# Storing a result tile that lies in two batches: one transfer over both, or two transfers of 64 rows

## The chip, the cores and the metric

The kernel runs on one core of one Trainium2 chip. The metric is the device time of one execution in microseconds (us). The core has TensorE (PE, with its weight loads as PEld), VectorE (DVE), ScalarE (ACT), GpSimd (POOL) and SyncE (SP). SP computes nothing: here it issues transfers, in program order, to 16 DMA engines.

## The reference

Block-sparse attention over 4 batches, 8 heads, 768 positions of 64 values, in blocks of 32 positions, and then a feed-forward network on the 3072 x 512 result.

```python
scores = scale * np.matmul(q, k.transpose(0, 1, 3, 2))
mask = np.abs(blk_i - blk_j) <= window              # window = 1
mask = mask | (blk_i == 0) | (blk_j == 0) | (blk_i == n_blocks - 1) | (blk_j == n_blocks - 1)
for qb in range(n_blocks):
    for kb in sampled_blocks[qb]:                   # 3 sampled blocks for each block of queries
        mask[qb * block:(qb + 1) * block, kb * block:(kb + 1) * block] = True
scores = np.where(mask, scores, -1000000000.0)
attn = softmax(scores)                              # over the last axis
x = (attn @ v).transpose(0, 2, 1, 3).reshape(B * S, H * D)
h = x @ w_in                                        # 512 x 2048
g = np.where(h > 0.0, h, alpha * (np.exp(np.minimum(h, 0.0)) - 1.0))
return (g @ w_out).astype(np.float32)               # 2048 x 512
```

## The kernel before

The work is cut into 24 units of 128 rows, four blocks of 32 query rows each. There are three kinds. In 20 units two neighbouring blocks of one batch stand beside the same two blocks of the next batch ("two batches"): partitions 0 to 63 of a tile belong to one batch, 64 to 127 to the other. In 2 units all four blocks are of one batch. 2 special units hold the first and the last block of both batches, whose rows see all keys. `attention` makes the scores (`s`, line 788), the exponentials (`e`), their 16-bit high and low parts (`p`, lines 820 to 824), turns `p` round (`pT`, line 825) and multiplies by the values (`w` or `av`, line 837). The result, normalised, is turned round too (`xT`). `ffn` takes two units at a time: the first layer `h` (line 885), the ELU on ACT and DVE (`fe`, lines 893 to 897), `g`, the second layer `o` (line 908).

From unit 4 on the turning is done by DMA transposes (line 377), issued by SP like every load and store. Loads of queries (line 642), keys (578), values (590), staged values (730 and others) and the stores of results all stand in SP's one order.

The result of a unit leaves PSUM as `ro` (line 918, on ACT or DVE, whichever the planner takes) and is stored by `move` (lines 624 to 642). There is a single `ro` buffer, so the next `ro` waits until the store before has landed. The last unit's result uses a `fe` buffer instead. `far` is the output seen as batch, position, column; `tile_` is the 128 x 512 tile in fp32, 256 KB, with rows of 2 KB.

The first store is issued 202.5 us into the span of the profiled execution.

The order on all engines comes from a planner, `Plan.order`, before the program is built. It plays the program forward with a cost for each operation on each engine that may do it, and hands out operations by priority; what it takes for an operation's cost changes which one it hands out next. For a store it takes a cost on SP and 0.9 of DMA time (lines 920 and 921). The costs are the planner's own; they decide the order and nothing else.

Of the kernel before, what the change touches and what calls it, by code (L numbers as in the profile page):

```python
# [225 lines left out]
def kernel(  # L226
# [15 lines left out]
    BLK = 32  # L242
# [21 lines left out]
    plan = Plan(rooms)  # L264
# [6 lines left out]
    def buf(tag, shape, dtype, pool=None):  # L271
        def make():
            made[0] += 1
            return (pool or sb).tile(
                shape, dtype, tag=tag, bufs=rooms[tag], name=f"{tag}{made[0]}")
        return Buf(tag, make)
# [18 lines left out]
    def scaled(eng, dst, src, scale=1.0):  # L295
        if eng == "ACT":
            nc.scalar.activation(dst, src, AF.Copy, scale=scale)
        elif scale == 1.0:
            ENG[eng].tensor_copy(dst, src)  # L299
        else:  # L300
            ENG[eng].tensor_scalar(dst, src, scale, None, op0=ALU.mult)
# [319 lines left out]
    def unit(u):  # L621
        return units[u]

    def move(u, dram, tile_, store=False):

        g, i, blocks = unit(u)
        if store:
            far = dram.rearrange("(b t) e -> b t e", b=B)
        else:
            far = dram.rearrange("b h t d -> b t h d")  # L630
        b, two = 2 * g + blocks[0][0], blocks[0][0] != blocks[3][0]
        if i and not two:
            parts = [(far[b, i * BLK : (i + 4) * BLK], tile_)]
        elif i and store:
            parts = [(far[b : b + 2, i * BLK : (i + 2) * BLK], tile_)]
        elif i:
            parts = [(far[b + x, i * BLK : (i + 2) * BLK], tile_[64 * x : 64 * x + 64]) for x in range(2)]
        else:
            parts = [(far[2 * g + x, n * BLK : (n + 1) * BLK], tile_[BLK * j : BLK * (j + 1)])
                     for j, (x, n) in enumerate(blocks)]  # L640
        for a, b in parts:
            nc.sync.dma_start(a, b) if store else nc.sync.dma_start(b, a)
# [15 lines left out]
    def attention(u, t, via):  # L658
# [6 lines left out]
        s, n = buf("st2", [P, H, D], F32), buf("n2", [P, H, 2, D], F16)  # L665
        qT, qS = buf("qT", [P, H, P], F16), buf("qS", [P, H, P], F16)
        plan.add({"SP": 0.9 if i0 else 1.8}, tq - 3, lambda e: move(u, q, s.ap), new=[s], dma=1.45, name=f"q{u}")
        split(tq - 1, s, n, lambda: n.ap[:, :, 0, :], lambda: n.ap[:, :, 1, :], QS, True, f"q{u}")
        turn16(tq if u != 1 else t - 0.5, n, lambda: qT.ap, via[0], new=[qT], name=f"qt{u}", bank="s" if u else "o")
# [202 lines left out]
    def ffn(U, t):  # L872
        x = xT[U]
        os = [buf("o", [P, DM], F32, ps) for _ in range(2)]
        for f2 in range(NFC // 2):
            h, e32, g = buf("h", [P, 2, 2 * P], F32, ps), buf("fe", [P, 2, 2 * P], F32), buf("g", [P, 2, 2, 2 * P], F16)
            p0 = t + F2 * f2
            for a in range(2):
                def layer1(e, f2=f2, a=a, h=h):
                    w = wi[2 * f2 + a]  # L880
                    n = 0
                    for cc in range(NCC):
                        cs = slice(cc * P, (cc + 1) * P)
                        for wl, xl in ((0, 0), (0, 1), (1, 0)):
                            nc.tensor.matmul(  # L885
                                h.ap[:, a, :], lhsT=w[:, wl, cs], rhs=x.ap[:, xl, cc, :],
                                start=(n == 0), stop=(n == 3 * NCC - 1))
                            n += 1
                plan.add({"PE": 1.31}, p0 + 1.3 * a, layer1, r=[x, w_ready[2 * f2 + a]],
                         new=[h] if a == 0 else [], w=[h] if a else [], code=24, name=f"h{U}.{f2}")  # L890

            def act3(e, h=h, e32=e32):
                nc.vector.scalar_tensor_tensor(  # L893
                    e32.ap, h.ap, -IH * GS, e32.ap, op0=ALU.mult, op1=ALU.min)
            plan.add({"ACT": 0.57}, p0 + 2.6, lambda e, h=h, e32=e32: nc.scalar.activation(  # L895
                e32.ap, h.ap, AF.Exp, scale=IH), r=[h], new=[e32], name=f"a1{U}.{f2}")
            plan.add({"ACT": 0.68}, p0 + 2.6, lambda e, e32=e32: nc.scalar.activation(  # L897
                e32.ap, e32.ap, AF.Relu, bias=gs_col, scale=-GS), r=[e32], w=[e32], name=f"a2{U}.{f2}")
            plan.add({"DVE": 0.66}, p0 + 2.6, act3, r=[h, e32], w=[e32], port=False, name=f"a3{U}.{f2}")
            plan.add(CAST, p0 + 2.6, margin=MC, fn=lambda e, e32=e32, g=g: scaled(e, g.ap[:, 0], e32.ap), r=[e32], new=[g],  # L900
                     name=f"a4{U}.{f2}")
            plan.add(LO, p0 + 2.6, margin=MO, fn=lambda e, e32=e32, g=g: ENG[e].tensor_tensor(  # L902
                g.ap[:, 1], e32.ap, g.ap[:, 0], op=ALU.subtract), r=[e32, g], w=[g], name=f"a5{U}.{f2}")
            for m in range(2):
                def layer2(e, f2=f2, m=m, g=g, o=os[m]):
                    for f in (2 * f2, 2 * f2 + 1):
                        for n, (gl, wl) in enumerate(((0, 0), (0, 1), (1, 0))):
                            nc.tensor.matmul(  # L908
                                o.ap, lhsT=g.ap[:, gl, f % 2, m * P : (m + 1) * P], rhs=wo[f][:, wl, :],
                                start=(f == 0 and n == 0), stop=(f == NFC - 1 and n == 2))  # L910
                plan.add({"PE": 1.31}, p0 + LAG + 1.3 * m, layer2,
                         r=[g, w_ready[NFC + 2 * f2], w_ready[NFC + 2 * f2 + 1]] + [os[m]] * (f2 > 0),
                         new=[os[m]] if f2 == 0 else [], w=[os[m]] if f2 else [], code=12, name=f"o{U}.{m}.{f2}")
        for m, o in enumerate(os):
            p0 = t + F2 * (NFC // 2 - 1) + LAG + 1.3 * m + 0.5
            tag = "fe" if m and U == NU // 2 - 1 else "ro"
            ro = buf(tag, [P, DM], F32)
            plan.add({"ACT": 0.6, "DVE": 0.65}, p0, lambda e, o=o, ro=ro: scaled(e, ro.ap, o.ap, IO),
                     r=[o], new=[ro], port=False, name=f"ro{2 * U + m}")
            plan.add({"SP": 0.6}, p0, lambda e, u=2 * U + m, ro=ro: move(u, out, ro.ap, True),  # L920
                     r=[ro], dma=0.9, name=f"st{2 * U + m}")

    SHIFT = {"ACT": 0.6, "DVE": 0.7}
# [18 lines left out]
    for U in range(NU // 2):  # L942
        t = F0 + T * U
        for u in (2 * U, 2 * U + 1):
            at = t - LEAD + (T / 2 if U else NEXT) * (u % 2)
            if u == NUP:
                for c in range(NKC):
                    for x in range(2):
                        keys(1, x, c, at - K1 + c, "PE")
                for c in range(NKC):  # L950
                    values(1, c, at - V1 + 5 * c)
            attention(u, at, ("PE", 4, "PE") if u < NPE else (("DMA", "PE")[QP], PP if u < TURNED else 0, ("DMA", "PE")[XP]))
        ffn(U, t)
# [32 lines left out]
```

## Time and profile before

| | us |
|---|---|
| runs: median, lowest, highest of 3 | 816.0, 815.18, 816.61 |
| the profiled execution: its time, its span | 816.94, 814.7 |
| PE busy | 710.6 (87%) |
| DVE busy | 509.7 (63%) |
| ACT busy | 407.6 (50%) |
| POOL busy | 393.9 (48%) |

The span runs from the first to the last instruction of the profiled execution. The execution's own time is 2.2 us longer, and 0.9 us above the median of the runs.

### The profile page before, as it was taken

Reading aid. Unit: us, or ns where it says so; the run is one execution under the profiler, and the core shown is the slowest. Engines: PE = TensorE matmul, PEld = TensorE weight load, DVE = VectorE, ACT = ScalarE, POOL = GpSimd, SP = SyncE. Lnnn points to the kernel's source line nnn. Section 1 sums busy time; section 2 is a strip of 40 time slices with the busy share of each in tenths; the row PEclk is TensorE's granted clock in tenths of the full one; section 3 lists DMA queues with packets and bytes.
Section 4 is the critical chain, followed back from the end, with each engine's and each line's share of the span. In section 5 each row is a group of like instructions: output and inputs, shape, how many; then the busy total and the mean of one; then the engine's idle time right before and its main releaser. Section 6 shows DMA issues by size and latency. Waiting matters only on the chain.

```text
span 814.7 us, 26279 instructions
## 1 busy us (share of the span) xinstructions
PE 710.6 (87%) x11064; PEld 478.8 (59%) x11064; DVE 509.7 (63%) x851; ACT 407.6 (50%) x725; POOL 393.9 (48%) x601
## 2 busy tenths in 40 slices
PE   6445576999999998999899899998999979989993
PEld 3333454667667656567567557666666556656761
DVE  7688787888776855675377567567565456463210
ACT  4588767887546635454465335324434343332220
POOL 2587657686634345743455455535633344322220
PEclk7555577999999999999999999999999999999998
DMA  9898998887958798989748999889587499861000
GB/s 240 262 270 275 275 245 185 216 180 143 183 137 247 150 176 181 146 175 186 153 80 159 116 199 120 158 127 151 93 189 127 67 111 191 133 86 20 27 1 26
DMA packets 216405, 126.33 MB, mean 155 GB/s; under 512 B 173344, under 2 KB 193952, under 8 KB 216288
## 3 DMA queue, kind: packets, MB, share of 16 engines
q1 hardware_dynamic: 211008, 107.09, 68.5%
q0 software_dynamic: 5280, 17.58, 8.4%
q8 instruction: 86, 1.41, 0.8%
q14 instruction: 31, 0.25, 0.1%
HBM read 82.05 MB, written 13.21 MB: 117 GB/s over the span
## 4 chain that ended last, share of the span: by engine, by line
PE 58%; DMA 19%; DVE 7%; issue 6%; SPq 3%; ACT 3%; POOL 2%; POOLq 1%; another core or an unknown queue 1%; DVEq 0%; ACTq 0%
PE h L885 23%; PE o L908 23%; DMA pT<-p 10%; PE s L788 5%; PE w L837 3%; PE av L837 2%; DMA wo<-in_moe_w_out_dram 2%; DMA st<-in_k_dram 2%; PE av L385 1%; DMA out_dram<-ro 1%; DMA vd<-VT 1%; DMA st<-in_v_dram 1%; PE s L385 1%; SPq L377 1%; DMA VT<-vd 1%
## 5 line engine op out<-in xcount | busy, mean ns | idle before, releaser
L885 PE MATMUL h<-xT,wi 128*128 128x256 f16 x2304 | 285.0, 276 | 10.9 <-DVE fe L893 8.0
L908 PE MATMUL o<-wo,g 128*128 128x512 f16 x1152 | 276.5, 383 | 0.5 <-issue 0.5
L885 PEld LDWEIGHTS <-wi 128*128 128x128 f16 x2304 | 220.7, 99 | 61.3 <-issue 10.3
L908 PEld LDWEIGHTS <-g 128*128 128x128 f16 x1152 | 108.1, 98 | 111.3 <-issue 4.8
L822 POOL TENSOR_TENSOR p<-e,p 128x512 f16<-128x512 f32 x94 | 112.1, 1195 | 115.3 <-DVE p L299 61.3
L902 POOL TENSOR_TENSOR g<-fe,g 128x512 f16<-128x512 f32 x69 | 83.2, 1206 | 140.2 <-DVE g L299 121.5
L895 ACT ACTIVATE fe<-h 128x512 f32<-128x512 f32 x96 | 57.2, 596 | 165.8 <-PE h L885 163.1
L817 ACT ACTIVATE e<-s,m 128x256 f32<-128x256 f32 x208 | 86.2, 469 | 82.1 <-POOL p L822 42.6
L893 DVE SCALAR_TENSOR_TENSOR fe<-h,fe 128x512 f32<-128x512 f32 x96 | 65.9, 687 | 73.0 <-ACT fe L897 68.4
L757 POOL COPY kG<-kT 128x128 int32 x264 | 78.2, 339 | 52.1 <-PE s L788 29.8
L799 DVE TENSOR_REDUCE m<-s 128x2 f32<-128x512 f32 x104 | 70.1, 686 | 44.1 <-PE s L788 40.8
L735 POOL DMA_INDIRECT VT<-vd,idx x66 | 65.9, 999 | 27.9 <-issue 10.0
L837 PEld LDWEIGHTS <-pT 128*32 128x32 f16 x3456 | 42.9, 97 | 47.9 <-issue 32.1
L897 ACT ACTIVATE fe<-fe,gs 128x512 f32<-128x512 f32 x96 | 69.3, 722 | 2.4
L846 DVE TENSOR_REDUCE x<-w 128x130 f32<-128x260 f32 x64 | 27.3, 426 | 56.3 <-PE w L837 50.8
L788 PE MATMUL s<-kG,qT 128*32 128x160 f16 x704 | 45.5, 250 | 9.8 <-ACT e L817 6.0
L788 PEld LDWEIGHTS <-qT 128*32 128x32 f16 x1664 | 33.6, 101 | 31.1 <-issue 26.8
L788 PE MATMUL s<-kT,qS 128*32 128x96 f16 (+1 forms) x832 | 49.1, 227 | 0.9 <-issue 0.9
L788 PE MATMUL s<-kT,qT 128*32 128x96 f16 (+1 forms) x832 | 49.0, 228 | 1.0 <-issue 1.0
L299 DVE CAST p<-e 128x512 f16<-128x512 f32 x58 | 33.7, 584 | 24.2 <-DMA pT<-p 11.8
L788 PE MATMUL s<-kG,qS 128*32 128x160 f16 x704 | 44.6, 249 | 4.2 <-DVE qS L299 2.7
L837 PE MATMUL w<-VT,pT 128*32 128x65 f16 (+1 forms) x2048 | 34.4, 208 | 7.4 <-DMA pT<-p 7.1
(134 smaller groups left out, 818.9 us busy)
## 6 DMA issues: line engine op xcount, KB each, us to landing
VT<-vd SPq DMA_DIRECT2D x44, 195.0 KB
VT<-vd SPq DMA_DIRECT2D x22, 390.0 KB
wo<-in_moe_w_out_dram SPq DMA_DIRECT2D x12, 512.0 KB
out_dram<-ro SPq DMA_DIRECT2D x21, 256.0 KB
st<-in_q_dram SPq DMA_DIRECT2D x40, 128.0 KB
wo<-in_moe_w_in_dram SPq DMA_DIRECT2D x9, 512.0 KB
st<-in_moe_w_in_dram SPq DMA_DIRECT2D x7, 512.0 KB
VT<-vd SPq DMA_DIRECT2D x12, 260.0 KB
```

The source lines that it names most:

```text
L735: nc.gpsimd.indirect_dma_start(VT[0:96, 2 * vt.slot, xs[0] : xs[-1] + 1].rearrange("p b x -> p (b x)"), None, d.ap, bass.IndirectOffsetOnA ...
L757: nc.gpsimd.tensor_copy(dst[:, :, r * 16 : (r + 1) * 16], src[:, :, bass.ds(at[r], 16)])
L788: nc.tensor.matmul(dst, lhsT=qq.ap[:, h, j * BLK : (j + 1) * BLK], rhs=mv, start=first, stop=(y == 1 and qq is qS and o0 + w == 256))
L799: nc.vector.tensor_reduce(m.ap[:, 2 * c : 2 * c + 2] if sp else m.ap[:, 6:8], ss[c].ap, axis=AX.X, op=ALU.max, negate=True)
L817: nc.scalar.activation(e32.ap[:, y, :], ss[c].ap[:, y, :], AF.Exp, bias=m.ap[:, 6 + y : 7 + y])
L822: plan.add(LO, t + PITCH * hp + 1, margin=MO, fn=lambda e, e32=e32, p=p: ENG[e].tensor_tensor(p.ap[:, 1, :], flat(e32.ap), p.ap[:, 0, :], ...
L837: nc.tensor.matmul(av.ap[j * BLK : (j + 1) * BLK, y, v0:], lhsT=pts[c].ap[:, pl * 4 + y * 2 + z, j * BLK : (j + 1) * BLK], rhs=VT[:, room, ...
L885: nc.tensor.matmul(h.ap[:, a, :], lhsT=w[:, wl, cs], rhs=x.ap[:, xl, cc, :], start=(n == 0), stop=(n == 3 * NCC - 1))
L893: nc.vector.scalar_tensor_tensor(e32.ap, h.ap, -IH * GS, e32.ap, op0=ALU.mult, op1=ALU.min)
L897: plan.add({"ACT": 0.68}, p0 + 2.6, lambda e, e32=e32: nc.scalar.activation(e32.ap, e32.ap, AF.Relu, bias=gs_col, scale=-GS), r=[e32], w=[ ...
L902: plan.add(LO, p0 + 2.6, margin=MO, fn=lambda e, e32=e32, g=g: ENG[e].tensor_tensor(g.ap[:, 1], e32.ap, g.ap[:, 0], op=ALU.subtract), r=[e ...
L908: nc.tensor.matmul(o.ap, lhsT=g.ap[:, gl, f % 2, m * P : (m + 1) * P], rhs=wo[f][:, wl, :], start=(f == 0 and n == 0), stop=(f == NFC - 1 ...
```

## The change

`move` loses its case for a store of a unit in two batches. Such a store then goes the way that the loads of such a unit always went: two transfers of 64 rows, one for each batch, issued one behind the other. The planner's cost of a store on SP goes from 0.6 to 1.1, for all kinds of units.

```diff
         if i and not two:
             parts = [(far[b, i * BLK : (i + 4) * BLK], tile_)]
-        elif i and store:
-            parts = [(far[b : b + 2, i * BLK : (i + 2) * BLK], tile_)]
         elif i:
             parts = [(far[b + x, i * BLK : (i + 2) * BLK], tile_[64 * x : 64 * x + 64]) for x in range(2)]
         else:
...
-            plan.add({"SP": 0.6}, p0, lambda e, u=2 * U + m, ro=ro: move(u, out, ro.ap, True),
+            plan.add({"SP": 1.1}, p0, lambda e, u=2 * U + m, ro=ro: move(u, out, ro.ap, True),
                      r=[ro], dma=0.9, name=f"st{2 * U + m}")
```

The lines after the first edit stand two lines higher in the changed file, so that line 642 becomes 640 and line 730 becomes 728.

What stands in SP's order, at three places. First, SP at the first store of a unit in two batches (`vd` holds the staged values in DRAM, `VT` those in SBUF, `ro` the result). Before:

```order
L706 DMA VT<-vd_183 64x1040
L642 DMA out_dram<-ro_5378 2x64x512
L730 DMA VT<-vd_175 96x1040
L730 DMA VT<-vd_183 96x1040
L599 DMA vd_191<-st_4360 128x2080
```

And after:

```order
L704 DMA VT<-vd_183 64x1040
L640 DMA out_dram<-ro_5378 64x512 x2
L728 DMA VT<-vd_175 96x1040
L728 DMA VT<-vd_183 96x1040
L599 DMA vd_191<-st_4360 128x2080
```

One issue has become two, and nothing else has moved here. Up to the tenth store of such a unit (at 501.87 us in the trace) the order on every engine is as it was.

Second, SP at and behind that tenth store, before:

```order
L377 DMA_TRANSPOSE pT_11036<-p_10981 128x8x128
L642 DMA out_dram<-ro_11056 2x64x512
L730 DMA VT<-vd_191 96x2080
L377 DMA_TRANSPOSE pT_11148<-p_11054 128x8x128
L377 DMA_TRANSPOSE xT_10598<-xn_11132 128x8x128
L377 DMA_TRANSPOSE pT_11293<-p_11195 128x8x128
```

And after:

```order
L377 DMA_TRANSPOSE pT_11044<-p_10989 128x8x128
L640 DMA out_dram<-ro_11064 64x512 x2
L377 DMA_TRANSPOSE pT_11121<-p_11062 128x8x128
L728 DMA VT<-vd_191 96x2080
L377 DMA_TRANSPOSE xT_10605<-xn_11157 128x8x128
L377 DMA_TRANSPOSE pT_11299<-p_11204 128x8x128
```

The transpose that stood behind the value load now stands ahead of it. From here on the planner's order differs in places on all five engines.

Third, SP at the loads of the second special unit, before:

```order
L377 DMA_TRANSPOSE pT_12980<-p_12923 128x8x128
L703 DMA VT<-vd_191 128x2080 x4
L377 DMA_TRANSPOSE xT_12960<-xn_13159 128x8x128
L703 DMA VT<-vd_191 128x2080
L705 DMA VT<-vd_191 64x2080
L706 DMA VT<-vd_191 64x2080
L642 DMA out_dram<-ro_13111 2x64x512
```

And after:

```order
L377 DMA_TRANSPOSE pT_12981<-p_12932 128x8x128
L640 DMA out_dram<-ro_13095 64x512 x2
L701 DMA VT<-vd_191 128x2080 x4
L377 DMA_TRANSPOSE xT_12978<-xn_13185 128x8x128
L701 DMA VT<-vd_191 128x2080
L703 DMA VT<-vd_191 64x2080
L704 DMA VT<-vd_191 64x2080
```

The store that stood behind seven value loads and a transpose now stands ahead of them.

## Rows read from the trace of the kernel before

**Rows 1.** The page: the busy time of each engine (with its share of the span and its instructions), and the shares of the chain that ended last, by engine.

```profile
PE 710.6 (87%) x11064; PEld 478.8 (59%) x11064; DVE 509.7 (63%) x851; ACT 407.6 (50%) x725; POOL 393.9 (48%) x601
PE 58%; DMA 19%; DVE 7%; issue 6%; SPq 3%; ACT 3%; POOL 2%; POOLq 1%; another core or an unknown queue 1%; DVEq 0%; ACTq 0%
```

**Rows 2.** Busy time by stretch: the stretch, its length, then busy us and instructions of PE, PEld, DVE, ACT and POOL, the granted clock of PE, the share of the 16 DMA engines that was busy, and GB/s.

```profile
200.00:500.00 300.00, 283.65 (x4635) 190.93 (x4633) 192.95 (x336) 148.00 (x265) 145.28 (x224) 0.99 0.86 160
500.00:803.00 303.00, 289.39 (x3999) 189.04 (x3997) 155.72 (x256) 111.01 (x206) 118.37 (x145) 0.99 0.65 104
803.00:813.50 10.50, 0.00 (x0) 0.00 (x0) 0.00 (x0) 0.00 (x0) 0.00 (x0) 0.67 0.13 47
```

**Rows 3.** SP's last two issues (start, length of the issue), both stores of units in two batches, and SP's last wait at the program's end (us in total, times, longest).

```profile
800.68 0.52 SPq L642 DMA_DIRECT2D out_dram<-ro  x1
802.04 0.52 SPq L642 DMA_DIRECT2D out_dram<-fe  x1
...
SPq L981 <- DMA out_dram<-fe: 5.1, 1, 5.1
```

**Rows 4.** Two stores of 256 KB side by side. The first is the special unit's, in four transfers of 32 rows: SP's issue of the four, the stretch 759.5 to 762 (columns as in rows 2), and in it the DMA share in 40 slices and the queue's packets, MB and share.

```profile
759.00 1.74 SPq L642 DMA_DIRECT2D out_dram<-ro  x4
759.50:762.00 2.50, 2.50 (x25) 2.24 (x24) 0.00 (x0) 0.00 (x0) 0.00 (x0) 1.00 0.40 105
DMA  0000095893205559621057973305389521000000
q1 hardware_dynamic: 192, 0.26, 40.1%
```

**Rows 5.** The second is the next one, of a unit in two batches in one transfer, issued at 762.87: the stretch 763.9 to 770.4 and its queue. The last line is the DMA share in 40 slices from 813.0 to 814.7, behind the last store of the program.

```profile
763.90:770.40 6.50, 6.50 (x56) 5.24 (x55) 3.25 (x6) 2.64 (x4) 2.36 (x3) 1.00 0.14 43
q1 hardware_dynamic: 130, 0.26, 12.5%
DMA  0202020200000000000000000000000000000000
```

**Rows 6.** SP's issues behind two such stores, in order of time (start, length of the issue), and the issue of all transposes of `p` (least, median, most ns; first and last start).

```profile
448.76 0.60 SPq L642 DMA_DIRECT2D out_dram<-ro  x1
449.46 5.17 SPq L377 DMA_TRANSPOSE pT<-p  x1
...
501.87 0.59 SPq L642 DMA_DIRECT2D out_dram<-ro  x1
...
503.06 5.80 SPq L377 DMA_TRANSPOSE pT<-p  x1
...
L377 SPq DMA_TRANSPOSE pT<-p x72: 1231/1408/6158, 160.9 to 731.2; - x72
```

**Rows 7.** Transfers in the chain that ended last (start of the issue, us until it had landed): a transpose with no store just ahead, two with one, a store for which the next `ro` waited, and two loads behind a store.

```profile
644.94 3.65 DMA pT<-p
650.57 10.23 DMA pT<-p
503.06 11.74 DMA pT<-p
373.62 9.46 DMA out_dram<-ro
388.22 9.39 DMA st<-in_k_dram
261.69 9.19 DMA st<-in_v_dram
```

**Rows 8.** PE's idle times that end with something late behind a store, in order of time (idle time and what ended it in brackets).

```profile
272.56 0.53 PE L837 MATMUL av<-VT,pT 128*32 128x130 f16 x32 [0.59 <-ACT pT L297]
389.74 0.62 PE L385 MATMUL s<-ident,n 128*128 128x128 f16 x8 [0.64 <-DVE n L497]
399.11 0.62 PE L385 MATMUL s<-ident,n 128*128 128x128 f16 x8 [3.09 <-DVE n L497]
463.22 0.53 PE L837 MATMUL w<-VT,pT 128*32 128x130 f16 x32 [3.38 <-DMA pT<-p]
514.84 0.53 PE L837 MATMUL w<-VT,pT 128*32 128x130 f16 x32 [0.74 <-DMA pT<-p]
568.48 0.54 PE L837 MATMUL w<-VT,pT 128*32 128x130 f16 x32 [1.38 <-DMA pT<-p]
660.85 0.71 PE L837 MATMUL av<-VT,pT 128*32 128x130 f16 x32 [2.79 <-DMA pT<-p]
718.15 1.25 PE L885 MATMUL h<-xT,wi 128*128 128x256 f16 x5 [3.17 <-DVE fe L893]
726.07 0.53 PE L837 MATMUL w<-VT,pT 128*32 128x130 f16 x32 [0.47 <-DMA pT<-p]
```

**Rows 9.** Waits for the `ro` buffer, from 200 us on, in total, times, longest; then DVE around one of them.

```profile
DVE ro L301 <- DMA out_dram<-ro: 22.6, 5, 8.9
ACT ro L297 <- DMA out_dram<-ro: 4.7, 2, 2.8
...
715.87 0.69 DVE L301 TENSOR_SCALAR ro<-o 128x512 f32<-128x512 f32 x1 [5.13 <-DMA out_dram<-ro]
...
717.41 0.68 DVE L893 SCALAR_TENSOR_TENSOR fe<-h,fe 128x512 f32<-128x512 f32 x1
```

**Rows 10.** SP's longest wait for another engine (us in total, times, longest).

```profile
SPq L377 <- POOL p L822: 87.1, 35, 8.3
```

## The prediction, made before the changed kernel had run

> **What bounds the kernel now.** I began with the busy times. PE works 710.6 us of 814.7, and the chain that ended last runs on PE for 58% of the span, on DMA for 19% and on no other engine for more than 7% [rows 1]. So only what makes PE wait, or what stands before its first or behind its last matmul, is worth anything. Stores begin at about 200 us. From there to 803 us PE is busy for 283.65 of 300 and 289.39 of 303 us at a granted clock of 0.99 of 2.4 GHz [rows 2]: some 30 us of idle time is left in the middle, which is all that a better order of transfers could win there. Behind 803 us no engine computes, the DMA engines are 0.13 busy at 47 GB/s, and SP waits for the last store [rows 2, 3]. That tail is the first thing to see.
>
> The second is why it is slow. Two stores of 256 KB stand within 4 us of each other. The special unit's, in four transfers of 32 rows, keeps 0.40 of the DMA engines busy over 2.5 us and is through by the 34th of 40 slices, at 761.6, which is 2.6 us behind its first issue at 759.00 [rows 4]. The next one, of a unit in two batches, carries the same 0.26 MB at 43 GB/s with a share of 0.14 for 6.5 us [rows 5]. A share of 0.13 to 0.14 of 16 engines is about two engines. I read it so: a transfer whose outer dimension is the two batches is dealt to two engines, 64 rows of 2 KB to each, while one whose outer dimension is rows is dealt to many.
>
> The third is what this does to others. SP's transfers queue behind one another, and a DMA transpose needs all the engines that it is dealt to. The transpose behind the store at 448.76 takes SP 5.17 us to issue, the one behind the store at 501.87 takes 5.80; the median is 1.41 [rows 6]. A transpose with no store just ahead landed 3.65 us after its issue, two behind a store 10.23 and 11.74; loads behind a store took 9.19 and 9.39 [rows 7]. The store itself keeps the only `ro` buffer for up to 9.46 us [rows 7], and DVE and ACT stood still for it for 22.6 and 4.7 us in all [rows 9].
>
> **The change, part by part.** *Tail.* Before: the last issue is at 802.04, the last packets are in slice 8 of 40 from 813.0 to 814.7, so at 813.3, and the span ends at 814.7, 1.3 us later [rows 3, 5]. Both of the last two stores share the two engines. After: two issues of 0.44 us each (four take 1.74 [rows 4]), the second at 802.5. In the four-part store the fourth issue begins 0.44 before the end of the 1.74, at about 760.3, and the last packet is at 761.6, so 1.3 us later; a part of 64 rows has twice the bytes, for which I add 0.2. The last packet is then at 804.0, the end at 805.4: 9.3 us earlier. Bounds: nothing, if 64 rows were also dealt to two engines, and 9.7 if the parts land as fast as those of 32 rows and overlap fully.
>
> *Middle.* Nine idle times of PE end with something late behind such a store: 0.59, 0.64, 3.09, 3.38, 0.74, 1.38, 2.79, 3.17 and 0.47, together 16.25 us [rows 8]. Three examples. At 463.22 PE waits 3.38 us for the transpose issued at 449.46 right behind a store. At 660.85 it waits 2.79 for the one that took 10.23. At 718.15 it waits for `fe`; DVE makes that at 717.41, because it stood 5.13 us for `ro` until the store before had landed [rows 9]. With the store through in 2.6 us instead of 7.5 or more, each of these transfers or buffers comes some 5 to 6 us earlier, more than any of the idle times. So the stores stop being the reason for all nine; what is late next is the ordinary chain from scores to `p` on DVE, ACT and POOL, for which SP's transposes already wait 87.1 us [rows 10]. I take three quarters of 16.25, 12.2 us, because a part will come back as waits for that chain. Bounds: nothing, and 22 (all nine and part of the other 14 us of idle time, where loads and transposes also crowd).
>
> *Second issue on SP.* 20 stores by 0.44 us are 8.8 us of SP. They lie beside the time that SP saves: 3.8 and 4.4 us over the median on each of the two transposes shown [rows 6]; and where no transpose follows, SP is waiting anyway [rows 10]. Cost taken: nothing beyond the 0.44 in the tail. Without that cover it would be 8.8 us at most.
>
> *The planner's cost.* 1.1 for 0.6 alone changes the order, and only from 501.87 us on. The swaps shown are a transpose ahead of a value load and a store ahead of seven value loads; the second lets `ro` go sooner and holds up the loads by 0.9 us of issue. PE's sum of work is the same. I take nothing, with 4 us to either side, about the longest single idle time (3.38) and a little.
>
> Sum, against the profiled execution: 816.9 - 9.3 - 12.2 = 795.4; it ran 0.9 above the median, so 794.5 for the median of runs, 21.5 us under the 816.0 before.
>
> **Two rules beside the rows.** Rows 4 show four parts of one store through in 2.6 us together, rows 5 one undivided store in 7.5. The Trainium skill's page SBUF — State Buffer, section The DMA setup-cost knee, speaks against this change: each transfer pays about 2 us whatever its size, so one should coalesce into the largest transfer possible. By it alone the second transfer would cost the tail 2 us where the rows give a gain of 9.3; no row here shows such a cost for parts that are issued back to back. On the spread, rows 5 show about two engines for two batches. The page DMA: Bandwidth & Descriptors, section Why a DMA increments its semaphore by 16 and not by 1, says that the number of engines is the largest up to 16 that divides the slowest dimension of both sides. By that it is 16 for 64 rows, which no store of 64 rows here shows; the share of 0.13 agrees with the 2 that it gives for two batches.
>
> **The rivals.** (a) Only the tail is won. For it: the 30 us of the middle lie in waits of at most 3.4 us [rows 8], and the DMA share there is 0.86 and 0.65 [rows 2], so transposes may crowd each other without any store. Against it: transposes with and without a store ahead differ by 7 us [rows 7]. Time: 816.0 - 9.3 = 806.7. (b) Everything goes: the nine waits and a third more, since loads and transposes elsewhere queue for the same DMA engines. Time: 816.0 - 9.3 - 22 = 785. Against it: four of the nine waits end with DVE or ACT, which have other work too [rows 8]. (c) The split does not spread. If each part of 64 rows falls to one engine of its own, nothing changes but the 0.44 of the second issue. If both parts fall to the same one, 256 KB at half of 47 GB/s take 11.2 us in place of 5.6 [rows 2]: the two stores of the tail need 22 us from 802 on and the end comes near 826, 11 us later; the middle's 16.25 us double. Time: 816 + 11 + 16 = 843. It decides as soon as the two parts share fewer than two engines. Against it: parts of 32 rows reach 0.40 of the engines [rows 4]. (d) The parts land one after the other, 1.3 us each. The tail then gains 8.0, and the seven waits for `ro` [rows 9] give 1.3 us back each, 9.1 of the 12.2. Time: 816.0 - 8.0 - 3.1 = 805. This is what the rule on coalescing would do here; at the page's 2 us it would be 810. Against it: rows 4. (e) The planner's order costs more than the rest brings: the store that now stands ahead of the special unit's loads makes these late, and PE waits for values. It needs 21.5 us of new waits, over six times the longest now, and decides from there. Time: 818.
>
> **How the numbers follow.** The forecast 0.60 (788 to 801), (a) 0.17, (b) 0.10, (c) 0.04, (d) 0.04, (e) 0.05. The likeliest gives 794.5. The range 785 to 807 holds the forecast, (a) and (d) and the upper half of (b); it leaves out (c), (e) and some of (b), together under 2 in 10. A change of 0.2%, 1.6 us, is about what a measurement of this kernel can tell from none. The forecast, (a), (b) and (d) are faster: 0.91. (c) and (e) hold the other 0.09: the same 0.03, slower 0.06.
>
> **What would show it.** After: behind the last matmul some 4 us to the end instead of 13; the issue of that store at 16 engines' share well over 0.13; the wait of DVE and ACT for `ro` near nothing; the longest issues of transposes on SP near 2 to 3 us instead of 6.2; no PE wait of 3 us for `pT` behind a store. The forecast is wrong if the tail's share stays at 0.13, or if PE's idle time between 200 us and its last matmul stays near 30 us, then as waits for `p`, for code or for value loads.

## The result, and the profile after

The changed kernel took 782.9 us, median of 4 runs (781.8 to 786.0), against 816.3 for the kernel before (median of 4): a ratio of 0.959, with a 95% interval of 0.956 to 0.963. That is 33.4 us less, where 21.5 were forecast, and 2 us under the lower end of the range. The direction was right, the size was not.

The first lines of the page after: busy time by engine, and the shares of the chain that ended last (of before in [rows 1]).

```profile
span 780.8 us, 26302 instructions
PE 703.2 (90%) x11064; PEld 476.2 (61%) x11064; DVE 504.7 (65%) x849; ACT 406.1 (52%) x723; POOL 398.8 (51%) x605
PE 80%; issue 4%; DMA 4%; DVE 4%; ACT 3%; POOL 3%; POOLq 1%; SPq 1%; another core or an unknown queue 1%; ACTq 0%; DVEq 0%
```

DMA has gone from 19% of the chain to 4%, and PE from 58% to 80%. PE also has 7.4 us less busy time for the same 11,064 matmuls; I come back to that.

Stretches of the two kernels, in the columns of [rows 2]: before, from 200 us to its last matmul; after, from 200 us to its last matmul; after, behind its last issue but one.

```profile
200.00:801.30 601.30, 573.03 (x8632) 379.97 (x8629) 348.67 (x591) 258.42 (x470) 263.65 (x368) 0.99 0.75 132
```

```profile
200.00:775.80 575.80, 565.73 (x8592) 377.94 (x8589) 342.09 (x585) 255.08 (x464) 268.46 (x372) 1.00 0.69 138
776.50:780.50 4.00, 0.00 (x0) 0.00 (x0) 0.00 (x0) 0.00 (x0) 0.00 (x0) 0.89 0.53 120
```

Length less PE's busy time is PE's idle time in the middle: 28.3 us before, 10.1 after. In the tail the DMA engines are 0.53 busy, where they were 0.13 [rows 2]. The traces' records of single packets say the same. Before, from 803.0 us to the last packet, just two packets of 2 KB are under way at a time for 9.5 of 10.2 us; after, from 776.0 us on, it is 13 or more for 2.0 of 2.9 us. The records name no engine, so "two engines" stays a reading, but one that fits share, rate and packets.

The span is the time to the last matmul and what follows. Before, 814.7 is 801.3 and 13.4; after, 780.8 is 775.8 and 5.0. So of the 33.9 us of the span 8.4 are the tail, 18.2 are idle time of PE behind 200 us, and 7.4 are PE's busy time; ahead of 200 us idle time changed by 0.1 (200 less 137.55 before, less 137.46 after).

SP's last issues after (of before in [rows 3]):

```profile
775.17 1.11 SPq L640 DMA_DIRECT2D out_dram<-ro  x2
776.52 1.29 SPq L640 DMA_DIRECT2D out_dram<-fe  x2
```

SP's last wait after (us in total, times, longest):

```profile
SPq L979 <- DMA out_dram<-fe: 1.4, 2, 0.8
```

The DMA share after, in 40 slices from 776.5 to 780.8:

```profile
DMA  5992796893569959505989772000000000000000
```

The last packet is in slice 25, at 779.2, which is 2.7 us behind the first issue of that store. SP waits 1.4 us for it instead of 5.1.

PE's waits after, from 200 us on (what waited, for what, us in total, times, longest):

```profile
PE av L385 <- issue: 3.3, 1, 3.3
PE s L786 <- issue: 1.9, 4, 0.5
PE s L385 <- ACT e L815: 1.6, 1, 1.6
PE w L786 <- ACT e L815: 1.2, 1, 1.2
PE s L786 <- ACT e L815: 1.2, 2, 0.9
PE h L883 <- issue: 0.3, 1, 0.3
```

No line names a DMA, and none names `fe` or `n` (a loaded tile of keys in its 16-bit parts). All nine waits of [rows 8] are gone. The groups that these nine belong to, before, from 200 us on:

```profile
PE w L837 <- DMA pT<-p: 7.1, 5, 3.4
PE h L885 <- DVE fe L893: 3.9, 2, 3.2
PE s L385 <- DVE n L497: 3.7, 2, 3.1
PE av L837 <- DMA pT<-p: 2.8, 1, 2.8
```

DVE's and ACT's 27.3 us of waiting for `ro` to land [rows 9] have no line any more either. SP's issues behind the store that was at 501.87 before [rows 6]:

```profile
487.48 1.17 SPq L640 DMA_DIRECT2D out_dram<-ro  x2
488.73 1.31 SPq L377 DMA_TRANSPOSE pT<-p  x1
```

The issues of all transposes of `p` after, in the columns of [rows 6]:

```profile
L377 SPq DMA_TRANSPOSE pT<-p x72: 1231/1274/5198, 158.6 to 707.7; - x72
```

The transpose right behind this store takes 1.31 us to issue instead of 5.80. Behind 200 us, 23 transposes took over 3 us to issue before, and 4 do after. The longest still takes 5.2 us, at 592.18; it stands behind value loads. The two issues of a store take 1.17 together, so the second costs SP about 0.6, not 0.44.

### The profile page after: what moved, and what is told of

It is laid out like the page before. It is cut to its first block, busy times and chain, and to the rows that moved or that the text cites. A ratio compares the mean times of both kernels' runs of the same rounds, so it can differ in the third digit from the quotient of the medians.

```text
span 780.8 us, 26302 instructions
## 1 busy us (share of the span) xinstructions
PE 703.2 (90%) x11064; PEld 476.2 (61%) x11064; DVE 504.7 (65%) x849; ACT 406.1 (52%) x723; POOL 398.8 (51%) x605
## 4 chain that ended last, share of the span: by engine, by line
PE 80%; issue 4%; DMA 4%; DVE 4%; ACT 3%; POOL 3%; POOLq 1%; SPq 1%; another core or an unknown queue 1%; ACTq 0%; DVEq 0%
PE o L906 32%; PE h L883 31%; PE s L786 6%; PE w L835 4%; PE av L835 2%; PE s L385 2%; DMA wo<-in_moe_w_out_dram 2%; ACT e L815 1%; PE av L385 1%; POOLq L751 1%; DMA VT<-vd 1%; POOL kG L755 1%; DMA raw<-in_sampled_blocks_dram 1%; POOL kG L748 1%
## 5 line engine op out<-in xcount | busy, mean ns | idle before, releaser
L883 PE MATMUL h<-xT,wi 128*128 128x256 f16 x2304 | 281.6, 275 | 4.7 <-DVE fe L891 4.0
L900 POOL TENSOR_TENSOR g<-fe,g 128x512 f16<-128x512 f32 x75 | 90.0, 1200 | 150.8 <-DVE g L299 134.8
L733 POOL DMA_INDIRECT VT<-vd,idx x66 | 64.5, 977 | 25.1 <-issue 10.1
L299 DVE CAST p<-e 128x512 f16<-128x512 f32 x59 | 32.0, 546 | 13.3 <-DMA pT<-p 6.1
L786 PEld LDWEIGHTS <-qS 128*32 128x32 f16 x1664 | 34.5, 102 | 6.0 <-DVE qS L299 3.0
```

The costliest lines, as they stand in the source:

```text
L733: nc.gpsimd.indirect_dma_start(VT[0:96, 2 * vt.slot, xs[0] : xs[-1] + 1].rearrange("p b x -> p (b x)"), None, d.ap, bass.IndirectOffsetOnA ...
L786: nc.tensor.matmul(dst, lhsT=qq.ap[:, h, j * BLK : (j + 1) * BLK], rhs=mv, start=first, stop=(y == 1 and qq is qS and o0 + w == 256))
L883: nc.tensor.matmul(h.ap[:, a, :], lhsT=w[:, wl, cs], rhs=x.ap[:, xl, cc, :], start=(n == 0), stop=(n == 3 * NCC - 1))
```

## The experiments

The theory: an undivided store is dealt to two DMA engines and holds up what queues behind it and what waits for its buffer; the split cures this by spreading the store. The rivals: the planner's new order brought part of it; it helps that a store comes in two smaller transfers, whatever the engines; each transfer has a price that is not hidden. Each ratio below is to runs of the kernel before on the same chip. Kernels that are compared by absolute times ran on one chip; the chips differ (last section).

**The split alone (e1_split) and the planner's cost alone (e2_cost).** The first makes the first edit of the change, the second the other:

```diff
-        elif i and store:
-            parts = [(far[b : b + 2, i * BLK : (i + 2) * BLK], tile_)]
```

```diff
-            plan.add({"SP": 0.6}, p0, lambda e, u=2 * U + m, ro=ro: move(u, out, ro.ap, True),
+            plan.add({"SP": 1.1}, p0, lambda e, u=2 * U + m, ro=ro: move(u, out, ro.ap, True),
```

> The split alone: stores of units in two batches go in two transfers of 64 rows, the planner's cost stays 0.6, so the order on every engine is that of the kernel before. The change took 33.4 us off, the forecast 21.5. Theory A (the spread of a store over the DMA engines is the whole cause): 783, within 3 us, with PE's idle time behind 200 us near 10 us as after the change. Theory B (the planner's new order from 501.87 us on brought the 10 us or so beyond the forecast): 790 to 796, with idle time of PE or a higher busy sum of PE left behind 500 us.

> The planner's cost of 1.1 alone: the order is that of the changed kernel, the store stays one transfer over both batches. Theory A: 816, within 4 us, with the tail of 13 us as before. Theory B: 804 to 809, some 10 us less than before.

Measured: the split alone 787.8 us, ratio 0.9645 (0.961 to 0.968); the cost alone 827.9 us, ratio 1.013 (1.010 to 1.016). The split alone, from 200 us to its last matmul:

```profile
200.00:782.20 582.20, 571.94 (x8631) 380.43 (x8629) 347.49 (x590) 258.67 (x470) 263.79 (x368) 0.99 0.70 136
```

787.8 lies between the two forecasts, 2 us above the one and 2 below the other; the profile decides. Idle time is 10.3 us, as after the change, with the order of before. So the split by itself takes out the whole 18 us. Of the waits for `ro` one stays (us in total, times, longest):

```profile
DVE ro L301 <- DMA out_dram<-ro: 8.9, 1, 8.9
```

Before, the same wait ended at 762.15, and it was for the special unit's store, which goes in four transfers in both kernels. The split does not touch it; it went with the new order, and with the split alone PE does not wait for it. The cost alone makes the kernel 1.3% slower, which neither theory had. Its stretch from 200 us to its last matmul:

```profile
200.00:814.80 614.80, 579.66 (x8594) 383.69 (x8591) 335.26 (x586) 256.09 (x465) 268.20 (x372) 0.98 0.73 129
```

PE's waits for transposes in it (us in total, times, longest):

```profile
PE w L837 <- DMA pT<-p: 11.9, 4, 3.9
PE av L837 <- DMA pT<-p: 4.5, 2, 2.6
```

SP and PE at its ninth store of a unit in two batches, the second place of the order shown above (the store at 501.87 before; it is the ninth, not the tenth):

```profile
504.79 0.59 SPq L642 DMA_DIRECT2D out_dram<-ro  x1
505.48 4.40 SPq L377 DMA_TRANSPOSE pT<-p  x1
...
517.72 0.85 PE L837 MATMUL w<-VT,pT 128*32 128x130 f16 x32 [3.92 <-DMA pT<-p]
```

Idle time is 35.1 us, 6.9 more than before. PE's busy time is 6.6 more, for which the clock is reason enough: behind 200 us eight stretches, 30.7 us together, have a granted clock of half, where before three have, 10.2 us. At this place the new order puts the transpose straight behind the store, where a value load stood between, and PE waits 3.92 us for it; in the order of before it was 0.74 [rows 8]. PE's waits for transposes come to 16.4 us in all, 9.9 before. The new order is worse as long as a store blocks what follows it.

**The tail alone (e3_tail) and the middle alone (e4_middle).** The split for the last two stores, and for all others:

```diff
-        elif i and store:
+        elif i and store and u < NU - 2:     # e3_tail
+        elif i and store and u >= NU - 2:    # e4_middle
```

> The split for the last two stores of the program alone, order as before. In the profiles the time from PE's last matmul to the end went from 13.3 to 5.0 us, so 8.4 us less: 808 by both theories, if the tail is a term of its own. If some of the 8.4 us comes back, 810 to 814.

> The split for all stores of units in two batches but the last two, order as before. Theory A: the middle's gain alone, 816.3 - 33.4 + 8.4, so 791, within 3 us. Theory B: 799 to 804, as the forecast's 12.2 us for the middle would have it. The tail stays at 13 us by both.

Measured: the tail 809.2 us, ratio 0.992 (0.989 to 0.995), 6.5 us; the middle 795.0 us, ratio 0.975 (0.972 to 0.978), 20.2 us. From 200 us to the last matmul, first the tail's kernel, then the middle's:

```profile
200.00:799.50 599.50, 573.10 (x8633) 380.91 (x8630) 345.36 (x591) 258.80 (x471) 262.97 (x371) 0.99 0.75 133
```

```profile
200.00:779.00 579.00, 568.45 (x8630) 378.93 (x8627) 347.71 (x590) 257.50 (x469) 263.86 (x368) 1.00 0.70 137
```

Idle time is 26.4 with the tail alone and 10.6 with the middle alone. In its profile the middle alone has 17.7 us less idle time than before and 4.6 us less busy time of PE. 0.992 times 0.975 is 0.967, and the split alone has 0.9645: the two terms add up. The tail came out 2 us under what the profiles give, with 8.4 still inside its interval; the middle's 795.0 is 1 us above theory A's range and 4 below theory B's, and its idle time is A's.

**How many engines, or how many transfers (e8_rows, e5_cols, e15_cols, e7_four).** One transfer of 128 rows, two transfers that are both over both batches, and four of 32 rows:

```diff
+        parts = [(dram[u * P : (u + 1) * P, :], tile_)] if store else parts     # e8_rows
...
-            parts = [(far[b : b + 2, i * BLK : (i + 2) * BLK], tile_)]
+            parts = [(far[b : b + 2, i * BLK : (i + 2) * BLK, c : c + 256], tile_[:, c : c + 256]) for c in (0, 256)]     # e5_cols, e15_cols
...
+            parts = [(far[b + x, (i + y) * BLK : (i + y + 1) * BLK], tile_[64 * x + 32 * y : 64 * x + 32 * y + 32])
+                     for x in range(2) for y in range(2)]     # e7_four
```

> One transfer of 128 rows for every store, to 128 rows of the output that follow one another (rows of a unit in two batches and of a special unit so stand elsewhere in the output than the reference has them; the bytes and the number of rows are the same). Order as before. Theory A: as good as the split or better by the second issues, 784 to 789, with the tail at 5 us or less. Rival C (two smaller transfers are what helps): 814 to 818.

> Two transfers for each store of a unit in two batches, but each still over both batches, with 256 of the 512 columns. Order as before. Theory A (what counts is how many DMA engines a transfer is dealt to, and the outer dimension of two sets that): no gain, 814 to 820, the tail still 13 us or more at a DMA share near 0.13. Rival C (what counts is that a store comes in two smaller transfers): 787 to 792, as with the split by rows.

> Two transfers of 256 columns each, over both batches, again. First measured at 0.991, on a chip whose runs of the kernel before lay between 806 and 818. If a store in two halves helps by itself, 0.988 to 0.994 again; if that was the chip, 0.997 to 1.004.

> Four transfers of 32 rows for each store of a unit in two batches. Order as before. Theory A with issues hidden on SP: within 2 us of the split alone (787.8), the tail longer by the two more issues, 0.9 us. Rival D (each transfer has a price on SP that is not hidden): 40 more issues by 0.44 us, up to 18 us more, 795 to 806.

Measured, all but e15_cols on one chip, on which the kernel before took 808.7: one transfer of rows 767.6 us, ratio 0.949 (0.943 to 0.954); two by columns 803.0 us, 0.991 (0.987 to 0.994), and again on another chip 0.998 (0.995 to 1.000); four 768.4 us, 0.951 (0.945 to 0.956). The tail of the kernel with columns, and of the one with one transfer of rows:

```profile
791.50:801.00 9.50, 0.00 (x0) 0.00 (x0) 0.00 (x0) 0.00 (x0) 0.00 (x0) 0.65 0.14 47
```

```profile
762.40:766.40 4.00, 0.00 (x0) 0.00 (x0) 0.00 (x0) 0.60 (x1) 0.00 (x0) 1.00 0.34 131
```

767.6 and 768.4 are some 16 to 21 us under what was expected of them; the expectations came from figures of other chips, and on a third chip the split alone takes 767.6 too (e14_split). One transfer that is not split gains all of it, as long as rows are its outer dimension. Its rows also lie side by side in the output; those of four transfers of 32 rows lie in two batches as before, and they gain as much. Two transfers with the batches as outer dimension stay at two engines' share, 0.14 and 47 GB/s. The 0.9% that these had at first was not there the second time. So it is the spread, not the number of transfers. Four transfers show no price of 18 us; 40 more issues on SP are hidden.

**Off SP's order (e6_actq).** The undivided store is issued by ACT:

```diff
-            nc.sync.dma_start(a, b) if store else nc.sync.dma_start(b, a)
+            (nc.scalar if len(parts) == 1 and two else nc.sync).dma_start(a, b) if store else nc.sync.dma_start(b, a)
```

> The undivided store over both batches is issued by ACT and not by SP, so no load or transpose stands behind it in SP's order; it is still dealt to two DMA engines, and the next ro still waits for its landing. Order as before. If the stall is that of SP's order alone, the middle's gain comes (795 to 799, tail still 13 us), less some us for 20 issues on ACT. If it is the two engines being taken, whoever issues, or the wait for ro: 812 to 820.

Measured: 817.6 us, ratio 1.011 (1.005 to 1.018), a little slower than before. Waits of DVE and ACT for `ro`, and of PE, in total, times, longest:

```profile
DVE ro L301 <- DMA out_dram<-ro: 29.8, 5, 8.9
ACT ro L297 <- DMA out_dram<-ro: 14.0, 3, 8.5
ACT fe L897 <- DVE ro L301: 4.1, 1, 4.1
...
PE h L885 <- DVE fe L893: 7.3, 3, 4.2
PE s L788 <- ACT e L817: 6.8, 2, 4.7
PE av L837 <- DVE pT L299: 4.8, 1, 4.8
...
PE w L837 <- DMA pT<-p: 0.7, 1, 0.7
```

PE's wait for transposes has all but gone, from 8.8 us in the five lines of [rows 8] to 0.7. In their place stand waits for `fe`, `e` and `pT` from DVE and ACT, and PE's idle time behind 200 us is 27.8 us (28.3 before). ACT now waits for DVE's `ro`, 4.1 us at one place, since the store of that `ro` stands in ACT's order. Both still wait for the landing, 43.8 us instead of 27.3. So leaving SP's order helps the transposes, but not the buffer, and it puts new waits on an engine that computes. It tells the two ways apart only in part.

**The two engines taken, `ro` free sooner (e13_aside, with e14_split beside it).** To the split is added, behind each of the 18 stores ahead of the last two, an undivided transfer that nobody waits for:

```diff
+    aside = nc.dram_tensor("aside", [B * S, DM], F32)
...
+        if store and i and two and u < NU - 2:
+            nc.sync.dma_start(aside.ap().rearrange("(b t) e -> b t e", b=B)[2 * g : 2 * g + 2, i * BLK : (i + 2) * BLK],
+                              wi_all[:, 0].bitcast(F32).rearrange("p a b -> p (a b)"))
```

> The split alone, and behind each of the 18 split stores ahead of the last two a transfer of 256 KB over both batches, from a tile of weights to a DRAM tensor that nobody reads; nothing waits for it. So two DMA engines are taken for as long as by the undivided store, 18 times, and ro is free as early as with the split. Order as before. If the transposes and loads queued behind are the larger way, most of the middle's 20 us is lost again: 798 to 808 where the split alone has 785 to 788. If the hold on ro is the larger way: 786 to 793.

> The split alone on the same chip, a ratio of 0.961 to 0.965 on the chips so far.

Measured: the split alone 767.6 us, ratio 0.951 (0.947 to 0.955); with the transfers aside a median of 822.1 us, ratio 1.020 (1.015 to 1.025). The four runs of the latter lie far apart, 811.2, 820.5, 823.6 and 826.0; those of the kernel before lie between 802.1 and 817.9, with a median of 809.0. The profile is of the run at 811.2. PE's waits for transposes in it, and DVE's for `ro`:

```profile
PE w L841 <- DMA pT<-p: 13.1, 6, 4.0
PE av L841 <- DMA pT<-p: 3.3, 2, 2.7
...
DVE ro L302 <- DMA out_dram<-ro: 12.9, 2, 8.9
```

SP at one of these transfers:

```profile
494.69 1.18 SPq L643 DMA_DIRECT2D out_dram<-ro  x2
495.92 0.56 SPq L645 DMA_DIRECT2D aside<-wi  x1
496.58 0.56 SPq L734 DMA_DIRECT2D VT<-vd  x1
497.24 4.60 SPq L378 DMA_TRANSPOSE pT<-p  x1
```

The transpose behind takes 4.60 us to issue, and PE waits 16.4 us for transposes, where it waited 9.9 before and not at all with the split alone. All of the gain goes, beyond both expectations: 767.6 us becomes at least 811.2. Whether the kernel is then slower than before is unclear, as the runs scatter so. The waits for `ro` are 16.6 us (12.9 on DVE, 3.7 on ACT) instead of 27.3, 8.9 of them the special unit's. So transfers on two engines that no buffer waits for bring back all that the undivided store cost, with more than half of the hold on `ro` gone. Two things are not shown: how much the hold on `ro` adds by itself, and how much of the loss is the 256 KB and the issue that each of the 18 transfers adds. No run adds the same bytes with rows outermost.

**Order and number again, on one chip (e9_after, e10_split, e11_four, e12_four_cost).** The changed kernel, the split alone, four transfers, and four transfers with the planner's cost of 1.1:

> The changed kernel again, beside the split alone on one chip, to tell what the planner's cost of 1.1 is worth once the stores are split. First measured at a ratio of 0.959 to the kernel before. If the new order is worth the 5 us by which it led the split alone, a ratio 0.006 below that of e10_split; if that was scatter between executions (lower granted clock in a few stretches of 3.4 us), within 0.002.

> The split alone again, order as before; first measured at 0.9645. See e9_after.

> Four transfers of 32 rows, order as before, on the same chip as the split in two. It came out at 0.9505 on another chip than the split in two. If four transfers are really better, a ratio at least 0.005 below e10_split; if the chips differ in how much they gain, within 0.003 of it, or above by up to 0.002 for the 40 more issues on SP.

> Four transfers of 32 rows with the planner's cost of 1.1. If order and number of transfers add up, e11_four less the gap between e10_split and e9_after, so the best of the four; if the order is worth nothing with split stores, equal to e11_four within 0.002.

| | median us | ratio to before, with its interval |
|---|---|---|
| the changed kernel | 782.8 | 0.9585 (0.954 to 0.963) |
| the split alone | 785.2 | 0.961 (0.957 to 0.966) |
| four transfers | 784.2 | 0.9585 (0.954 to 0.963) |
| four transfers, cost 1.1 | 781.5 | 0.956 (0.952 to 0.960) |

The order leads by 2.4 us with two transfers and by 2.6 with four, about 0.3%, between the two expectations. The intervals of the ratios overlap, but they hold the scatter of the kernel before, which is the same in both. The six runs set against the six give 2.4 us with an interval of 0.6 to 4.2 for two transfers, and 2.4 with 0.2 to 4.6 for four. So the lead is small, and just clear of the scatter. Four transfers are as good as two. Four with the cost of 1.1 has the lowest median, 1.3 us under the changed kernel, which is about the scatter.

## Why the prediction was wrong, point by point

**Tail: right in mechanism, a little high.** Forecast 9.3 us, by the profiles 8.4, measured alone 6.5 with an interval of about 4 to 9. The second issue is 0.6 us, not 0.44; the last packet comes 2.7 us behind the first issue where 2.0 were worked out, and the end 1.6 us behind that, not 1.3.

**Middle: a step that failed.** "I take three quarters of 16.25, 12.2 us, because a part will come back as waits for that chain." Idle time fell by 18.2 us in the profiles, 6.0 more than I took. The waits that name transposes, `fe`, `n` or `pT` were 18.1 us before and are nothing after: the nine, and two that I had not counted, 0.76 us for `fe` at 551.98 and 1.10 us for a transpose at 684.31. Something did come back, but only 2.0 us: PE's waits for `e` rose from 2.0 to 4.0, while those that end with "issue" fell from 7.7 to 5.5. What I took for the next limit, SP's wait for POOL's `p`, stayed (90.1 us, after 87.1), and no wait of PE names it. So the whole of the nine waits should have been taken, and the two like them.

The middle alone measured 20.2 us, close to the upper bound of 22 that I had set and given 0.10 as rival (b). But that is not rival (b)'s account: part of the 20.2 is busy time of PE, the next point.

**PE's busy time: the other step that failed.** "PE's sum of work is the same": I held its time constant with it, and it fell by 7.4 us, a term that the sum lacked. Either miss alone would have left the forecast inside its range, at 788.5 or 787.1; it took both. Part of the 7.4 is the clock. Before, three stretches behind 200 us ran at a granted clock of about half, so at 1.2 GHz; after, one. The columns are those of [rows 2]; first before, then after. (The DMA share counts the whole time of each packet that starts in the stretch, so in a short stretch it can pass 1.)

```profile
314.90:318.50 3.60, 3.59 (x29) 2.71 (x29) 1.72 (x3) 2.52 (x4) 0.00 (x0) 0.53 1.39 241
400.30:403.90 3.60, 3.60 (x14) 1.68 (x13) 2.55 (x5) 1.00 (x2) 3.05 (x8) 0.53 0.83 178
717.70:721.30 3.60, 3.15 (x16) 2.27 (x17) 3.50 (x5) 0.63 (x1) 2.45 (x2) 0.53 1.71 70
```

```profile
311.90:315.50 3.60, 3.60 (x40) 2.67 (x32) 2.79 (x6) 2.54 (x4) 0.00 (x0) 0.53 0.85 191
315.50:775.80 460.30, 455.68 (x6771) 303.87 (x6769) 264.88 (x452) 195.42 (x356) 215.67 (x301) 1.00 0.66 127
```

Each costs 3.6 by 0.47, 1.7 us of work at full clock. The one at 400 us begins 1.3 us behind the idle time of 3.09 us that ends at 399.11; the one at 717 begins in the last 0.3 us of the 3.17 that end at 718.15 [rows 8]. So with those two waits up to 3.4 us more than their length went away. The three slower kernels bear it out: e2_cost, e6_actq and e13_aside have 15 waits of PE between 3.1 and 4.8 us behind 200 us, and at 14 of them a stretch at half clock begins in the wait or within 1.4 us of its end. It is no rule: the longest wait before, 3.38 us at 463.22, has no such stretch, and profiles of the same order do not agree on how many there are.

The other 4 us are settled in part. If half of PE's busy time in stretches at half clock is taken off, its busy time behind 200 us is 568.5 us before, 567.5 with the split alone and 565.4 with the changed order, these two on one chip (e10_split, e9_after). By this estimate some 2 us come with the order; the rest is open.

**Second issue on SP: right.** It is hidden: twice as many transfers (e11_four) cost nothing that shows.

**The planner's cost: forecast at nothing within 4 us.** With split stores it is worth some 2 us, so right. That the same order alone costs 1.3% was not foreseen. Its worth depends on whether a store blocks what stands behind it.

**A sign and a reading that did not hold.** The longest issue of a transpose was to fall from 6.2 to 2 or 3 us and is 5.2. The 6.2 stood at 673.60, behind value loads as the 5.2 does, with no store just ahead of it. And of the 27.3 us of waiting for `ro` only 18.4, in six waits, were for undivided stores; the seventh was for the special unit's, as the split alone shows.

**Price of a transfer, and engines.** Two transfers of 128 KB were through in 2.7 us together, four of 64 KB in 2.6 [rows 4]. The rule of the Trainium skill's page SBUF — State Buffer, section The DMA setup-cost knee, about 2 us for each transfer, did not decide here. Shares were 0.13 and 0.14 wherever the outer dimension was two, and 0.34 to 0.53 wherever it was rows. The rule of the Trainium skill's page DMA: Bandwidth & Descriptors, section Why a DMA increments its semaphore by 16 and not by 1, which sets the number of engines by the slowest dimension of both sides, agrees with that.

## What to carry to other kernels

When the DMA engines' share in a stretch with one transfer is near one or two sixteenths, look at the transfer's outer dimension: here a transfer over two batches ran at two engines' share, and splitting it by batch, or putting rows outermost, spread it. Price such a transfer by what queues behind it, not by its own landing: here all nine waits of PE that ended behind one went in full, and with two of the three longest a stretch at half clock. What a planner's cost is worth can depend on the transfer's shape: the new order cost 1.3% with the undivided store and gained some 0.3% with the split one. Measure the two apart and together.

## What the runs showed of the hardware

The chips differ more than the terms at issue. The split alone took 787.8 and 785.2 us on two chips, and 767.6 on a third, where the kernel before took 816.1, 816.4 and 809.0; four transfers took 784.2 on one and 768.4 on another. Profiles of the kernels that gained most have next to no idle time left: from 200 us to the last matmul, with four transfers at 768.4, and with the same kernel at 784.2:

```profile
200.00:760.80 560.80, 559.54 (x8576) 375.05 (x8573) 344.36 (x583) 253.89 (x462) 263.07 (x366) 1.00 0.73 141
```

```profile
200.00:777.80 577.80, 568.82 (x8610) 378.75 (x8596) 346.24 (x588) 257.34 (x468) 264.68 (x368) 0.99 0.69 138
```

Idle time is 1.3 and 9.0 us. The waits that end with "issue", 3.3 us at one place after the change, are among those that the faster chip did not have. Why is open. The ratio to the kernel before is what can be compared, and that too moved, from 0.96 to 0.95.
